# First expert of a routed layer: its first 256 rows listed after one count step instead of three

## The chip, the cores and the metric

The kernel runs on one NeuronCore of a Trainium2 chip. TensorE (PE) multiplies matrices, VectorE (DVE), ScalarE (ACT) and GpSimd (POOL) work on tiles, SyncE (SP) issues plain DMAs; GpSimd issues the indirect DMAs that gather and scatter rows. Each engine takes its own instructions in the order of the program, and semaphores tie the engines together. The metric is the device time of one execution in microseconds.

## The reference

Windowed attention (8 sequences of 576 positions, 8 heads of 64, a window of 128 with a distance bias) gives x, 4608 rows of 512. Then comes a layer of eight experts with a fixed capacity:

```python
N, D = x.shape
E = w_gate.shape[1]
cap = N // E
logits = x @ w_gate
flat = logits.flatten()
order = np.argsort(-flat)
...
for idx in order:
    tok, e = (int(idx) // E, int(idx) % E)
    if assigned[tok] >= 0 or counts[e] >= cap:
        continue
    assigned[tok] = e
    counts[e] += 1
...
for e in range(E):
    mask = assigned == e
    h = np.maximum(x[mask] @ w1[e], 0.0)
    out[mask] = h @ w2[e]
```

All 36864 pairs of a row and an expert are taken in the order of their logits; a row goes to the first expert that still has room, and each expert takes exactly 576 rows. Which expert fills first, and with which rows, is known only when all logits are.

## The kernel before, in words

**Routing** runs in eight phases (`Router.phase`). A phase finds the threshold at which the next expert fills: rows are held as 36 columns of 128, each row has its best expert (`OH`) and its logit (`b`). A count step places the logits into 64 bins (`place` writes `kq`), compares them with 64 bin numbers (`indicate` writes `ind`), and TensorE counts the members of every expert at every bin (matmuls `m<-OH,ind`). `enough` turns the counts into the step (`odd`, `junk`, `mx`, `sat` on VectorE, then a matmul `m<-sat,c_ones`), and `lo`, `w` hold the narrowed interval. Phase 0 does three such steps, of which most of the first is counted during attention (only the last ten columns are left for its end). A matmul `m<-T,c_ones` then gives the totals of the experts (`Dc`), VectorE names the expert (`ei`), and the list of its 576 rows is made: running sums (`run`, `ex`), positions by two matmuls, one-hot codes (`hif`, `hv`, `hOH`, `slo`, `mv`, `loOH`), 18 matmuls `m<-mv,loOH`, and `io`, `ia`, `idx`. The later phases count candidates in another way (`few`, matmuls `m<-OHf,ind`) and end with the same list.

**An expert.** Five gathers of 128 rows (the last of 64) fetch x by `idx` (`g`). TensorE turns each tile (four transposes into `pg` or `po`: a flip), ScalarE casts it (`xh`) and VectorE takes the remainder (`xl`). The weights come as four chunks of 512 KB a layer (`raw`, four buffers). ScalarE casts each (`hl`, 1024 columns) and VectorE takes two remainders of 512 columns (`hl`; here called splits). Layer 1 multiplies xh by both parts of the weights and xl by the high part: 192 matmuls into `ph`; ScalarE applies the ReLU (`hh`) and VectorE takes its remainder (`hlo`, and a short `hh`). For the first expert layer 1 runs over columns 0 to 255 for all eight blocks of 128 hidden units and then over columns 256 to 575; the other experts take two halves of 288 together, block by block. Layer 2 has 112 matmuls into `po`, tile by tile; ScalarE copies the result and GpSimd scatters it.

**Order.** Routing of phase 0 is written in program order on VectorE and TensorE. Elsewhere a scheduler places instructions from the order in which the code was recorded. `slot` is called at the steps of a layer's generator and hands out routing steps, loads, splits and flips by the tables `W_LOAD` and `W_SPLIT`, so the routing of the next expert but one runs beside the layers of an expert. Around the first expert the order is set by `issue_after` and by zero matmuls (`keep_warm`, 24 of them), which occupy TensorE while it has nothing else. The request of the first expert's weights (`loads`) reads `ei` into a register of SyncE; chunks 2 and 3 wait for a copy `late` behind the first flips.

## Time and profile before

| | us |
|---|---|
| median of three runs | 691.48 |
| lowest and highest run | 691.15, 692.19 |
| the profiled execution | 692.76 |
| its span | 691.0 |
| first matmul of layer 1, first expert | 231.03 |
| first matmul of layer 1, second expert | 295.08 |

A row of the chain of waits gives the start, the duration and the work in it. A row of a timeline gives the start, the time, the engine, the line, the operation, what it writes and reads, shapes and a count; in brackets stands the engine's idle time before it and what ended that. Where a helper records every operation (the line L456 or, in the changed program, L461), one looks at the names of the tiles. The numbers behind a group of names are busy times, not intervals: matmuls overlap, so their mean time is longer than the step from one to the next.

### The profile page before, as it was taken

To read this page: it belongs to the slowest core of one execution; us is meant where nothing else is said; L and a number is where in the kernel's file an instruction comes from. 1 tells how busy PE (TensorE), PEld (TensorE's weight loads), DVE (VectorE), ACT (ScalarE), POOL (GpSimd) and SP (SyncE) were. 2 spreads that over 40 slices of the span, in tenths; PEclk is the share of its full clock that TensorE was granted. 3 is DMA by queue.
4 is the path that set the end of the run, shared out by engine and by line. 5 is a ranking of instruction groups with operands and counts; after the bars stand their busy time and mean duration, and the time that the engine had idled before them with its cause. 6 is when DMAs were issued, how large, how long until landed. Compare 5 with 4: busy or idle time off the path is not lost.

```text
span 691.0 us, 18850 instructions
## 1 busy us (share of the span) xinstructions
PE 660.8 (96%) x7266; PEld 581.2 (84%) x7267; DVE 453.4 (66%) x1876; ACT 325.1 (47%) x991; POOL 152.4 (22%) x337
## 2 busy tenths in 40 slices
...
GB/s 313 139 205 206 195 227 173 219 179 223 109 90 80 228 25 251 121 131 191 74 206 102 93 132 158 45 123 183 55 114 172 104 92 152 110 30 39 1 25 49
DMA packets 35138, 92.71 MB, mean 134 GB/s; under 512 B 3808, under 2 KB 13152, under 8 KB 35040
## 3 DMA queue, kind: packets, MB, share of 16 engines
...
q8 instruction: 59, 0.97, 0.6%
q14 instruction: 39, 0.32, 0.2%
...
## 4 chain that ended last, share of the span: by engine, by line
PE 85%; DVE 7%; DMA 4%; ACT 2%; issue 1%; SPq 0%; POOL 0%; POOLq 0%; DVEq 0%
PE ph L954 26%; PE po L983 10%; PE po L984 10%; PE po L986 8%; PE s L53 7%; PE x L53 7%; PE pt L53 7%; PE pt L160 6%; PE pg L931 2%; DMA raw<-in_w_dram 2%; DVE hl L898 1%; ACT hl L896 1%; ACT u L147 1%; PE m L589 1%; DMA rel_sb<-in_rel_dram 1%
## 5 line engine op out<-in xcount | busy, mean ns | idle before, releaser
L954 PE MATMUL ph<-xh,hl 128*128 128x288 f32 (+2 forms) x1024 | 189.8, 299 | 0.0
L954 PEld LDWEIGHTS ph<-xh,hl 128*128 128x128 f32 x1024 | 154.3, 189 | 1.0
L983 PE MATMUL po<-hl,hh 128*128 128x512 f32 (+1 forms) x328 | 130.8, 399 | 0.0
L147 ACT ACTIVATE u<-u,mn 128x192 f32<-128x192 f32 (+2 forms) x288 | 124.0, 438 | 5.5 <-DVE mn L137 5.5
L984 PE MATMUL po<-hl,hh 128*128 128x512 f32 (+1 forms) x328 | 126.5, 386 | 0.0
L954 PE MATMUL ph<-xl,hl 128*128 128x288 f32 (+2 forms) x512 | 115.7, 298 | 0.0
L960 ACT ACTIVATE hh<-ph 128x288 fp32r<-128x288 f32 (+2 forms) x128 | 46.8, 408 | 144.6 <-PE ph L954 144.3
L986 PE MATMUL po<-hl,hlo 128*128 128x512 f32 (+1 forms) x264 | 102.1, 387 | 0.0
L898 DVE TENSOR_TENSOR hl<-raw,hl 128x512 fp32r<-128x512 f32 x128 | 84.9, 682 | 13.7 <-ACT hl L896 13.2
L137 DVE CUSTOM_DVE_ANT_0 u<-s,bm 128x192 f32<-128x192 f32 (+1 forms) x248 | 71.8, 346 | 32.4 <-PE s L53 31.7
L995 POOL DMA_INDIRECT out_dram<-o,idx x40 | 44.6, 1116 | 204.2 <-ACT o L990 125.0
L954 PEld LDWEIGHTS ph<-xl,hl 128*128 128x128 f32 x512 | 84.1, 189 | 0.1
L935 DVE TENSOR_TENSOR xl<-pg,xh 128x512 fp32r<-128x512 f32 (+1 forms) x37 | 23.7, 640 | 83.0 <-ACT xh L934 82.9
L965 DVE SCALAR_TENSOR_TENSOR hlo<-ph,hh 128x288 fp32r<-128x288 f32 (+2 forms) x128 | 49.8, 417 | 39.7 <-ACT hh L960 39.5
L896 ACT CAST hl<-raw 128x1024 fp32r<-128x1024 f32 x64 | 65.5, 1049 | 17.1 <-DMA raw<-in_w_dram 12.1
L983 PEld LDWEIGHTS po<-hl,hh 128*128 128x128 f32 x328 | 61.8, 188 | 11.1
L984 PEld LDWEIGHTS po<-hl,hh 128*128 128x128 f32 x328 | 61.9, 189 | 10.6
L990 ACT COPY o<-po 128x512 f32<-128x512 f32 (+1 forms) x33 | 18.9, 573 | 95.5 <-PE po L986 60.5
L907 POOL DMA_INDIRECT g<-x,idx x40 | 43.4, 1086 | 83.4 <-PE pg L931 33.8
L53 PE MATMUL s<-qk 64*64 64x192 f32 (+1 forms) x992 | 60.5, 327 | 0.6 <-DMA qk<-in_qk_dram 0.3
L986 PEld LDWEIGHTS po<-hl,hlo 128*128 128x128 f32 x264 | 49.6, 188 | 10.1
L147 ACT ACTIVATION_READ_ACCUMULATOR u<-u,mn 128x1 f32 x288 | 55.8, 194 | 0.0
...
## 6 DMA issues: line engine op xcount, KB each, us to landing
...
g<-x,idx POOLq DMA_INDIRECT x40, 3.4
out_dram<-o,idx POOLq DMA_INDIRECT x40, 2.8
```

The costliest lines, as they stand in the source:

```text
L53: put(nc.tensor.matmul(out, w, a, start=start, stop=stop, skip_group_check=True))
L137: put(nc.vector.tensor_tensor_reduce(out=weights(n, t, h), in0=x[:, c:c + 64 * m].rearrange("q (j k) -> q j k", k=64), in1=bm[n % NP][:, y ...
L147: put(nc.scalar.activation(u, u, AF.Exp, bias=st["mn"][:, i:i + 1], scale=-1.0, accum_out=st["sm"][:, i:i + 1]))
L896: self.last = nc.scalar.copy(hl[:, 0, :], raw)
L898: nc.vector.tensor_tensor(hl[:, 1, c:c + 512], raw[:, c:c + 512], hl[:, 0, c:c + 512].bitcast(F32), ALU.subtract)
L954: nc.tensor.matmul(pp[t], w[:, a, j, fo:fo + 128], x[:, j, cut[t]:cut[t + 1]], start=(j == 0 and a == 0 and x is xh), stop=(j == 3 and a = ...
L960: nc.scalar.activation(o, pp[t], AF.Relu)
L965: nc.vector.scalar_tensor_tensor(d, pp[t][:, c0:c1], 0.0, o[:, c0:c1].bitcast(F32), ALU.max, ALU.subtract)
L983: nc.tensor.matmul(out, a, wh, start=(f == 0), stop=False)
L984: nc.tensor.matmul(out, a, wl, start=False, stop=(f == 7 and t == 4))
L986: nc.tensor.matmul(out, hl[:, f, 128 * t:128 * t + 128], wh, start=False, stop=(f == 7))
L995: self.sent = nc.gpsimd.indirect_dma_start(out=self.out, out_offset=bass.IndirectOffsetOnAxis(ap=idx[:r, t:t + 1], axis=0), in_=o[:r, :], ...
```

## The change

The changed program makes two lists for the first expert. After the first of the three count steps, `first_full` takes the expert whose count stays at 576 or more up to the highest bin as the guess, and the rows of it that lie above that bin within the first 28 columns; the first 256 of these are listed (`idxa`). With the guess in a register of SyncE three chunks of weights are requested, and two gathers fetch the 256 rows. The other two count steps follow; what they select, less the rows listed already (`rest`), gives a second list of 320 rows for three more gathers. Layer 1 runs first over the 256 columns, then over the 320, and layer 2 over all five tiles. A flag is set if the second list has not exactly 320 rows or if the expert is another; then the exact path computes everything over again. VectorE, TensorE and ScalarE get their order from the program in this part (`OrderedCore` with `scalar`), in layer 2 TensorE alone (`OrderedTensor`). The routing of the second expert starts in the second half of layer 1 and runs in layer 2 by the table `ROUTE_2`, in 40 steps of layer 2; its gathers are issued at step 30 and its flips stand at steps 36, 37, 38 and 40. The routing of the third expert starts with the second expert. There are 13 zero matmuls instead of 24. The diff, cut to its core:

```diff
-EARLY = 4
-AHEAD = (18, 0, 0)
-EARLY0 = 1
-SOON, HI0 = 2, 1
+AHEAD = 18, 0, 0
+ZEROS = 1, 4, 1, 3, 4
+CHOICE_1 = {1: 1, 4: 1, 6: 1}
+LOWS_2 = {3: 2, 5: 2, 6: 2, 7: 2}
+ROUTE_2 = 11, 13, 15, 17, 19, 21, 22, 25, 29
+GATHER_2, TURN_2 = 30, (36, 37, 38, 40)
+LOAD_2 = {24: 2, 30: 1, 34: 1}
+SPLIT_2 = 33, 35, 37, 39
...
+AHEAD_COLS, AHEAD_ROWS = 28, 256
...
+    def first_full(self, cnt, more, key, am, w, low):
+        nc, rt, C = self.nc, self.p["rt"], self.C
+        n = AHEAD_COLS
+        odd, total = rt.tile([J, 8], F32, name="odd"), rt.tile([J, 8], F32, name="junk")
+        nc.vector.tensor_tensor(odd, cnt[J:2 * J, 8:16], more[J:2 * J, :], ALU.add)
+        nc.vector.tensor_tensor(total, cnt[0:J, 0:8], odd, ALU.add)
+        full = rt.tile([J, 8], BF, name="fo", bufs=1)
+        nc.vector.tensor_scalar(full, total, float(CAP), None, ALU.is_ge)
+        g = self.bank()
+        nc.tensor.matmul(g[:, 0:8], C["ones"][0:J, :], full, start=True, stop=True)
+        lo2, top, sg, mx, v = (self.small(name, k) for name, k in (("lo", 1), ("top", 1), ("sg", 8), ("kmx", 1), ("of", 1)))
+        nc.vector.tensor_reduce(top, g[:, 0:8], AX.X, ALU.max)
+        nc.vector.scalar_tensor_tensor(sg, g[:, 0:8], 8.0, C["e8"], ALU.mult, ALU.add)
+        sel = rt.tile([128, NT], BF, name="sel")
+        nc.vector.tensor_scalar(sel[:, 0:n], key[:, 0:n, 0], top[:, 0:1], None, ALU.is_ge)
+        nc.vector.tensor_reduce(mx, sg, AX.X, ALU.max)
+        nc.vector.scalar_tensor_tensor(v, top, -8.0, mx, ALU.mult, ALU.add)
+        m, ex = self.members(am, v[:, 0:1], sel, n)
+        nc.vector.tensor_scalar(self.guess, v, -1.0, 8.0, ALU.mult, ALU.add)
+        nc.vector.scalar_tensor_tensor(lo2, w, top[:, 0:1], low, ALU.mult, ALU.add)
+        return lo2, m, ex, v
+    def ahead_hits(self, m, ex):
+        nc, n = self.nc, AHEAD_COLS
+        sp = self.bank()
+        self.positions(sp, m, ex, n)
+        some = self.some = self.p["rt"].tile([128, NT], BF, name="some_m", bufs=1)
+        nc.vector.scalar_tensor_tensor(some[:, 0:n], sp[:, 0:n], float(AHEAD_ROWS), m[:, 0:n], ALU.is_lt, ALU.mult)
+        return self.hits(sp, some, n, 2, self.nc.scalar)
+    def ahead_rows(self, hits):
+        self.rows(self.bank(), hits, AHEAD_COLS, 2, self.few_rows)
+        r = self.rest[:, 0:AHEAD_COLS]
+        self.nc.vector.tensor_tensor(r, r, self.some[:, 0:AHEAD_COLS], ALU.subtract)
...
+        cnt = self.count(ind, OH, c0, NT)
+        w2, low = self.small("w"), self.small("low")
         nc.vector.tensor_tensor(low, lo, w, ALU.subtract)
         nc.vector.tensor_scalar(w2, w, 1.0 / J, None, ALU.mult)
+        self.place(cl, lo, rw, 0, c0, key)
+        rw2 = self.small("rw")
         nc.vector.tensor_scalar(rw2, rw, float(J), None, ALU.mult)
-        n = yield from n
-        lo2 = self.small("lo")
-        nc.vector.scalar_tensor_tensor(lo2, w, n[:, 0:1], low, ALU.mult, ALU.add)
-        return lo2, w2, rw2
+        lo, m, ex, v = self.first_full(cnt, self.part, key, am, w, low)
+        w, rw = w2, rw2
+        key = self.place(cl, lo, rw)
+        hits = self.ahead_hits(m, ex)
+        for s in (1, 2):
+            ind = rt.tile([128, NT, J], BF, name="ind", bufs=1)
+            for i, (a, z) in enumerate(self.halves(0, NT)):
+                if s == 1 and i == 0:
+                    self.indicate(ind, key, a, z)
+                    self.ahead_rows(hits)
+                    yield
+                else:
+                    self.indicate(ind, key, a, z)
+            low = self.small("low")
+            nc.vector.tensor_tensor(low, lo, w, ALU.subtract)
+            if s == 1:
+                w2, rw2 = self.small("w"), self.small("rw")
+                nc.vector.tensor_scalar(w2, w, 1.0 / J, None, ALU.mult)
+                nc.vector.tensor_scalar(rw2, rw, float(J), None, ALU.mult)
+            yield
+            cnt = self.count(ind, OH, 0, NT)
+            yield
+            n = self.enough(cnt, self.pen)
+            next(n)
+            yield
+            try:
+                next(n)
+            except StopIteration as e:
+                n = e.value
+            if s == 1:
+                lo2 = self.small("lo")
+                nc.vector.scalar_tensor_tensor(lo2, w, n[:, 0:1], low, ALU.mult, ALU.add)
+                lo, w, rw = lo2, w2, rw2
+                key = self.place(cl, lo, rw)
+        sel, rest = (rt.tile([128, NT], BF, name=name, bufs=1) for name in ("sel0", "rsel"))
+        nc.vector.tensor_scalar(sel, key[:, :, 0], 1.0, n[:, 0:1], ALU.add, ALU.is_ge)
+        nc.vector.tensor_tensor(rest, self.rest, sel, ALU.mult)
+        nc.vector.scalar_tensor_tensor(self.hi, w, n[:, 0:1], low, ALU.mult, ALU.add)
+        m, ex = self.members(am, v[:, 0:1], rest, NT)
...
+        idx = rs.tile([128, 5], I32, name="idx", bufs=4)
+        self.rows(self.bank(), hits, NT, 3, idx)
+        self.idx[0] = [self.few_rows[:, t:t + 1] for t in range(2)] + [idx[:, t:t + 1] for t in range(3)]
+        yield
...
+    go()
+    raw = ask(r.guess, 0, range(3))
+    rows = [r.few_rows[:, t:t + 1] for t in range(2)]
+    ga = m.gather(rows, range(2), m.x[0:128 * AHEAD_COLS, :])
+    m.idle = P["ps_h"].tile([128, 512], F32, name="ph")
+    W = [m.high(raw[c]) for c in range(2)]
+    go(2)
+    m.keep_warm(ZEROS[0])
+    m.low(W[0], raw[0], 0)
+    go()
+    m.keep_warm(ZEROS[1])
+    m.low(W[0], raw[0], 1)
+    go(2)
+    m.low(W[1], raw[1], 0)
+    a0 = m.flip(*ga[0], "o")
+    m.keep_warm(ZEROS[2])
+    go()
+    a1 = m.flip(*ga[1])
+    m.keep_warm(ZEROS[3])
+    go()
+    m.under(*a0)
+    m.under(*a1)
+    late = marked(0)
+    raw += ask(late, 0, (3,))
+    second = ask(late, 1, (0,))
+    m.keep_warm(ZEROS[4])
+    m.hidden()
+    go()
+    layer(0, 0)
+    m.low(W[1], raw[1], 1)
+    layer(1, 0)
+    W.append(m.high(raw[2]))
+    go()
+    gb = m.gather(r.idx[0], range(2, 5))
+    rest(0, 0)
+    go()
+    for half in range(2):
+        m.low(W[2], raw[2], half)
+    layer(2, 0)
+    W.append(m.high(raw[3]))
...
+    late = marked(1)
+    second += ask(late, 1, range(1, 4))
...
+    V, lows = [], []
+    for f in range(8):
+        layer(f, 1)
+        if f == 0:
+            go()
+        if f % 2 == 0:
+            V.append(m.high(second[f // 2]))
+            lows += [(V[-1], second[f // 2], half) for half in range(2)]
+        if f:
+            rest(f - 1, 1)
+        for _ in range(CHOICE_1.get(f, 0)):
+            next(route)
+        for _ in range(LOWS_2.get(f, 0)):
+            m.low(*lows.pop(0))
+    rest(7, 1)
+    return V
...
-    with tc.issue_after(r.last.ins):
-        for _ in range(EARLY0):
-            next(route)
-    W = {(0, 0): [m.split(raw[c]) for c in range(HI0)]}
-    with tc.issue_after(r.last_pe.ins):
-        m.idle = P["ps_h"].tile([128, 512], F32, name="ph")
-        m.keep_warm(WARM0)
-    tn = m.turn(g, True)
-    with tc.issue_after(m.last.ins):
-        next(tn)
-    with tc.issue_after(m.turned.ins):
-        late = P["rt"].tile([1, 1], I32, name="late")
-        last = tc.nc.vector.tensor_copy(late, r.ei[0][0:1, 0:1])
-    raw += list(m.loads(late, 0, range(SOON, 4)))
-    with tc.issue_after(m.last.ins):
-        for _ in range(TURN0 - 1):
-            next(tn)
-    W[0, 0] += [m.split(raw[c]) for c in range(HI0, 4)]
-    with tc.issue_after(last.ins):
-        for _ in range(EARLY - EARLY0):
-            next(route)
...
+        V = first_expert(tc, P, C, r, m, route)
+        r.nc = m.nc = OrderedTensor(tc)
+    i = 0
+    for _ in m.layer2(V, m.h, r.idx[0], fine=True):
+        i += 1
+        if i in ROUTE_2 and not exact:
+            next(route)
+        if i == GATHER_2:
+            gathers[0] = m.turn(m.gather(r.idx[1]))
+        for _ in range(LOAD_2.get(i, 0)):
+            load(1, 0)
+        if i in SPLIT_2:
+            part(1, 0)
+        if i in TURN_2:
+            next(gathers[0])
+    while len(W[1, 0]) < 4:```

Three places show how the order moves. On VectorE, behind the first count step, where `hl` is the split of a weight chunk of the first expert and `idxa` the early list; before:

```order
L456 TENSOR_SCALAR kq<-c_74,lo,rw 128x72
L456 TENSOR_TENSOR ind<-kq,c_i_425 128x1152 x2
L456 TENSOR_TENSOR low<-lo,w 128x1
L456 TENSOR_SCALAR w<-w 128x1
L456 TENSOR_SCALAR rw<-rw 128x1
L456 TENSOR_TENSOR odd<-m,pen 64x8
L456 ISA junk,mx<-m,odd 64x8
L456 ISA mx 64x1
L456 TENSOR_SCALAR sat<-mx 64x1
L456 SCALAR_TENSOR_TENSOR lo<-w,m,low 128x1
L456 TENSOR_SCALAR kq<-c_74,lo,rw 128x72
L456 TENSOR_TENSOR ind<-kq,c_i_425 128x1152 x2
```

and now:

```order
L461 SCALAR_TENSOR_TENSOR idxa<-ia 64x2 x2
L461 TENSOR_TENSOR rest<-rest,some_m 128x28
L461 TENSOR_TENSOR ind<-kq,c_i_429 128x1152
L461 TENSOR_TENSOR low<-lo,w 128x1
L461 TENSOR_SCALAR w<-w 128x1
L461 TENSOR_SCALAR rw<-rw 128x1
L461 TENSOR_TENSOR hl<-raw,hl 128x512
L461 TENSOR_TENSOR odd<-m,pen 64x8
L461 ISA junk,mx<-m,odd 64x8
L461 ISA mx 64x1
L461 TENSOR_SCALAR sat<-mx 64x1
L461 TENSOR_TENSOR hl<-raw,hl 128x512
```

Between the second count's indicators and its sum `odd` stands a split now, and another one between `sat` and the next `lo`.

On TensorE, at the end of the first expert's layer 2, where the flips of the second expert (`pg<-ident_sb,g`) stand; before, one flip and what follows it:

```order
L986 MATMUL po<-hl,hlo 128x512
L525 MATMUL m<-ed,craw 128x1
L931 MATMUL pg<-ident_sb,g 128x128 x4
L983 MATMUL po<-hl,hh 128x512
L984 MATMUL po<-hl,hh 128x512
L986 MATMUL po<-hl,hlo 128x512
```

and now:

```order
L461 MATMUL po<-hl,hh 128x512 x8
L461 MATMUL pg<-ident_sb,g 128x128 x4
L461 MATMUL po<-hl,hh 128x512 x2
L461 MATMUL pg<-ident_sb,g 128x128 x4
L461 MATMUL po<-hl,hh 128x512 x2
L461 MATMUL pg<-ident_sb,g 128x128 x4
L461 MATMUL po<-hl,hh 128x512 x4
L1105 MATMUL ph<-xh,hl 128x288
L461 MATMUL pg<-ident_sb,g 128x128 x4
```

The flips stood far apart, each followed by many matmuls of layer 2; now four of them stand within nine matmuls, the fourth one behind the first matmul of the second expert's layer 1.

On ScalarE, at the same place, where `hl` is the cast of a weight chunk of the second expert, four of layer 1 and then those of its layer 2, and `xh` the cast of a turned tile; before:

```order
L896 CAST hl<-raw 128x1024 x3
L990 COPY o<-po 128x512
L934 CAST xh<-pg 128x4x128
L896 CAST hl<-raw 128x1024 x2
L990 COPY o<-po 128x512
L934 CAST xh<-pg 128x4x128 x2
L990 COPY o<-po 128x512
L934 CAST xh<-pg 128x4x128
L990 COPY o<-po 128x512
L934 CAST xh<-pg 128x4x64
```

and now:

```order
L1036 CAST hl<-raw 128x1024 x3
L1154 COPY o<-po 128x512
L1036 CAST hl<-raw 128x1024
L1078 CAST xh<-pg 128x4x128
L1036 CAST hl<-raw 128x1024 x2
L1078 CAST xh<-pg 128x4x128
L1036 CAST hl<-raw 128x1024
L1078 CAST xh<-pg 128x4x128
L1036 CAST hl<-raw 128x1024
L1078 CAST xh<-pg 128x4x128
L1111 ACTIVATE hh<-ph 128x288
L1078 CAST xh<-pg 128x4x64
```

Two casts of layer-2 weights stood ahead of the second `xh`; now four stand ahead of the fourth, and the copies `o` of layer 2 are past.

421 lines of the change are left out of this document (267 added, 154 removed).

## The prediction

> **What bounds the kernel now.** I read the busy times and the chain of waits first, then the busy times by stage, and then the instructions between the last attention block and the first layer of the first expert, one engine at a time. The page's busy times (span 691.0 us) and its chain by engine:
>
> ```profile
> PE 660.8 (96%) x7266; PEld 581.2 (84%) x7267; DVE 453.4 (66%) x1876; ACT 325.1 (47%) x991; POOL 152.4 (22%) x337
> PE 85%; DVE 7%; DMA 4%; ACT 2%; issue 1%; SPq 0%; POOL 0%; POOLq 0%; DVEq 0%
> ```
>
> TensorE is the bound nearly everywhere, so only stretches in which it stands still have something to give. The windows by stage (all tiles; columns: PE, PEld, DVE, ACT and POOL busy with counts, then the granted clock, the DMA share and GB/s) show where these are:
>
> ```profile
> 207.00:208.00 1.00, 0.44 (x5) 0.29 (x5) 0.78 (x6) 0.00 (x0) 0.00 (x0) 0.62 1.01 286
> 208.00:224.00 16.00, 5.31 (x64) 3.28 (x66) 12.18 (x51) 1.58 (x2) 0.00 (x0) 0.50 0.22 74
> 224.00:225.00 1.00, 1.00 (x5) 0.43 (x4) 0.91 (x2) 0.93 (x2) 0.97 (x1) 0.84 0.02 8
> 231.00:295.00 64.00, 60.41 (x415) 51.97 (x412) 52.06 (x196) 26.36 (x42) 12.28 (x12) 1.00 0.45 154
> 295.00:354.00 59.00, 57.99 (x399) 50.14 (x397) 46.21 (x176) 18.63 (x34) 17.45 (x18) 1.00 0.38 131
> ```
>
> From 208 to 224 VectorE is busy for 12.18 of 16 us with the routing of the first expert while TensorE has 5.31. This is the hole that the change works on. Behind it the first expert takes 64 us (TensorE idle 3.59) and the second 59 (idle 1.01). These two are the cover that the change draws on: VectorE is already busy for 52.06 of the 64.
>
> The hole ends as the chain tells, where the last row is the first matmul of the second expert:
>
> ```profile
> 224.03 3.51 DMA g<-x,idx
> 227.59 0.67 PE pg L931 x4
> 295.08 2.60 PE ph L954 x19
> ```
>
> **The change part by part. (1) The early list.** Today three count steps come one after the other, and then the choice, the list, the gathers. The rows of VectorE:
>
> ```profile
> 208.38 0.15 DVE L456 TENSOR_SCALAR sat<-mx 64x1 bf16<-64x1 f32 x1
> 208.80 0.22 DVE L456 SCALAR_TENSOR_TENSOR lo<-w,m,low 128x1 f32<-128x1 f32 x1 [0.28 <-PE m L456]
> 209.06 0.32 DVE L456 TENSOR_SCALAR kq<-c,lo,rw 128x72 bf16<-128x72 f32 x1
> 209.41 1.43 DVE L456 TENSOR_TENSOR ind<-kq,c_i 128x1152 bf16<-128x1152 bf16 x2
> 217.91 0.15 DVE L456 TENSOR_SCALAR ei<-ef 128x1 int32<-128x1 f32 x1
> 219.05 0.20 DVE L456 TENSOR_SCALAR hif<-m 128x36 f32<-128x36 f32 x1 [0.34 <-PE m L456]
> 220.42 1.42 DVE L456 TENSOR_TENSOR loOH<-c_i,slo 128x1536 bf16<-128x1536 bf16 x2
> 222.73 0.33 DVE L456 SCALAR_TENSOR_TENSOR idx<-ia 64x5 int32<-64x5 f32 x2
> 226.43 0.68 DVE L898 TENSOR_TENSOR hl<-raw,hl 128x512 fp32r<-128x512 f32 x1
> 230.33 0.69 DVE L935 TENSOR_TENSOR xl<-po,xh 128x512 fp32r<-128x512 f32 x1 [0.15 <-ACT xh L934]
> ```
>
> and of SyncE (requests of weights), ScalarE, GpSimd (gathers) and TensorE:
>
> ```profile
> 219.10 12.72 SPq L889 DMA_DIRECT2D raw<-in_w_dram  x4
> 223.01 2.16 ACT L896 CAST hl<-raw 128x1024 fp32r<-128x1024 f32 x2 [2.28 <-DMA raw<-in_w_dram]
> 224.03 1.18 POOL L907 DMA_INDIRECT g<-x,idx  x1 [22.18 <-DVE L L456]
> 221.43 0.85 PE L456 MATMUL m<-mv,loOH 128*128 128x40 bf16 x18 [2.42 <-DVE loOH L456]
> 222.50 4.30 PE L915 MATMUL ph<-zero 128*128 128x512 bf16 x15 [0.22 <-issue]
> 231.03 0.72 PE L954 MATMUL ph<-xh,hl 128*128 128x256 f32 x4
> ```
>
> Up to 208.80 nothing changes in time. Then come eight short VectorE steps from `top` to `ex` (0.15 to 0.25 each with their starts about 0.2 apart, like the rows from `sat` to `kq`): 1.6 us, to 210.4. `guess` is ready at 210.55. From the end of `ei` (218.06) to the first weight cast (223.01) it is 4.95 us today, so the first cast can begin at 215.5, 7.5 us sooner. `lo` and `kq` follow to 211.05. From `hif` to the end of `loOH` it is 2.79 us today for 36 columns and five tiles. With 28 columns and two tiles the big step shrinks by 1792/2304 and the one-hot steps by two thirds: an estimate of 2.5 us with `some_m`, to 213.55. Fourteen matmuls instead of 18 are 0.66 us (0.85 x 14/18), the three steps to `idxa` 0.78 (today from 222.28, the end of the 18, to 223.06): 215.0. Today the gather starts 0.97 after `idx` ends (223.06 to 224.03), so it starts at about 216.0, and its rows can be turned at 219.5 (3.51 later) rather than 227.5.
>
> **(2) What holds the early start back.** The two other count steps now run behind this list, with weight splits between them. The second count's sum `odd` stands behind the first weight split, so it waits for a transfer, a new wait for VectorE's routing: cast 215.5 to 216.55, split 0.68, `odd` at 217.25 (its counts would be there at 216.2). `sat` 217.8, split 218.5, `lo`, `kq` and `ind` 220.45, TensorE's counts 220.9. Only behind these stand the two flips, so the gathers have 1.4 us in hand. A third split, `odd` to `sat` (221.7), six short steps to `ex` (223.2) and two xl of 0.69: 224.6. I take 225.0 for the first matmul, against 231.03: **6.0 us earlier**. Bounds: 222.6 if the casts come in time and two of the splits fall into waits, 227.6 if the weights come later by 2.6 (more than half of the 4.95).
>
> **(3) The first expert.** The matmuls of a layer, from windows of the experts six and seven taken for `ph` alone (first row) and for `po` alone (second):
>
> ```profile
> 526.00:580.00 54.00, 26.12 (x192) 1.00 0.38 120
> 526.00:580.00 54.00, 26.63 (x112) 1.00 0.38 120
> ```
>
> The halves of 256 and 320 columns are there today, so layer 1 stays at 26.1. Inside it now stand 18 matmuls of the second list, the totals and three flips: 0.65 (an estimate, under the 0.85 they take at half clock), 0.3 and 2.0 (0.67 each), in all 2.95. It ends at 254.05, routing of the second expert apart. Layer 2 finds its last two weight chunks not split yet, since VectorE has two halves left (2 x 0.68) and their casts: 1.8 us of waiting, bounds 0.5 and 3.5. The totals of the second expert's routing stand behind 66 of layer 2's 112 matmuls (15.7 us) and behind that routing's range and counts, 2.46 (a whole phase is 3.58 by the windows under (5); the totals, the positions and the list, which come later, are 0.3, 0.2 and 0.62 of it): 254.05 + 1.8 + 15.7 + 2.46 = **274.0**.
>
> **(4) From there to the second expert.** What follows the totals today, in the third expert's routing (first five rows), and the first and last of the second expert's five gathers:
>
> ```profile
> 298.75 0.30 PE L700 MATMUL m<-T,c_ones 128*128 128x288 bf16 x1
> 307.67 0.74 DVE L965 SCALAR_TENSOR_TENSOR hlo<-ph,hh 128x288 fp32r<-128x288 f32 x2
> 308.34 0.21 DVE L965 SCALAR_TENSOR_TENSOR hh<-ph,hh 128x64 fp32r<-128x64 f32 x1
> 309.78 0.33 DVE L756 SCALAR_TENSOR_TENSOR idx<-ia 64x5 int32<-64x5 f32 x2
> 310.88 1.49 POOL L907 DMA_INDIRECT g<-x,idx  x1 [8.67 <-PE ph L954]
> ...
> 267.33 1.04 POOL L907 DMA_INDIRECT g<-x,idx  x1 [7.39 <-issue]
> 273.87 0.91 POOL L907 DMA_INDIRECT g<-x,idx  x1 [0.31 <-issue]
> ```
>
> Today the second expert's gathers run from 267.33 to 273.87, and its layer 1 begins at 295.08: some 18 us in hand. In the changed program they come 12.1 us (298.75 to 310.88) after totals at 274.0, less 0.8: between the steps of the list VectorE has three splits there (3 x 0.68), where today it has three rounds of hidden-layer remainders (0.74 + 0.21 each, 2.85). First gather 285.3, last 291.8 (6.5 later), landed 295.3; flip, cast and split of the short tile take 1.2 (an estimate, from 0.67 and 0.69 of a full one): 296.5. TensorE's own work from the totals on is 10.9 (46 of 112 matmuls) + 0.8 (positions and list) + 3.0 (flips) = 14.7, so without waiting it would be through at 288.7. Twelve matmuls of the next layer 1 (1.6) can run before the last tile is there, so the second expert counts as begun at **294.9**, against 295.08. Of the 6.0 us, 5.8 are spent: the wait for weights and gathers that stood ahead of the first expert comes back ahead of the second. What is queued behind it: `xh` of tiles 1 to 4 stand on ScalarE behind casts of that expert's layer-2 weights, and so behind their transfers. I price this at nothing within those 6 us of waiting, and at 3 us (three casts of 1.05) as a bound.
>
> **(5) Routing that moves back.** The windows of the tile `m` on TensorE alone (routing matmuls):
>
> ```profile
> 231.00:295.00 64.00, 5.75 (x80) 1.00 0.45 154
> 295.00:354.00 59.00, 4.96 (x76) 1.00 0.38 131
> 354.00:412.00 58.00, 3.58 (x51) 1.00 0.41 133
> ```
>
> A whole phase costs 3.58; the first expert today holds 5.75, so 2.2 us of the third expert's routing are done there. In the changed program that phase begins with the second expert. The same 2.2 us then run after 295, and no cover exists for them, TensorE being the bound: **+2.2**. From the fifth expert on the order of TensorE is the same in both.
>
> **Sum.** -6.0 for the start; +5.8 for what is lost by the second expert's start; +2.2 for routing done later: **+2.0 us**. It is made against the profiled execution (692.76, span 691.0), 1.3 us over the median 691.48; taken over to the median, 693.5.
>
> [...] By the windows the granted clock is 0.50 from 207.24 (0.62 in its first microsecond) to 224.32 (0.84 in the last), 17.1 us, and then full. TensorE had then worked without a break since 221.43, the list and 15 of today's 24 zero matmuls. The changed program has 13, but counts, flips and list stand among them from about 216. [...]
>
> **The rivals.** *The early start is kept.* If the list of the second expert comes as soon as TensorE needs it, only the 14.7 us of work follow the totals, not 20.9 (294.9 - 274.0): 693.5 - 6.2 = 687.3 us. For it: half the gathers' path is VectorE work that could go faster than in the rows quoted, since layer 2 gives VectorE nothing else but splits, and layer 2's stall may be 0.5. Against it: gather, five issues and landing alone are 10 us (6.5 + 3.5) behind a list that needs the totals first. *The weights of the second expert decide.* Eight chunks through four buffers, each freed by its splits; the casts ahead of `xh` then add the 3 us above, and the counts in layer 2 stall as today, where TensorE waited for `ind`:
>
> ```profile
> PE m L589 <- DVE ind L565: 3.1, 2, 1.8
> ```
>
> One such wait, 1.8, comes on the path: 693.5 + 3 + 1.8 = 698.3 us. It decides as soon as a layer-2 chunk lands later than the third gather. *Half clock at the start*: today the clock was back 2.9 us after TensorE's unbroken work began (221.43 to 224.32). If that work begins only with layer 1 at 225.0, the first 2.9 us run at half and 1.4 are lost: 694.9. Against it: counts and flips stand close together before. *The guess is wrong.* Then the exact path runs the experts over again, at least another 460 us (231 to 691). With the reference's inputs the first expert to fill stays the first at the finer steps, 372 of its rows are sure in the first 28 columns, and 320 remain, so I give it 1 in 100.
>
> **How the numbers follow.** This kernel's measurements can tell about 0.2% (1.4 us) from no change. Forecast (most of the gain spent, between 690 and 696): 0.46, of which half within 0.2%. Early start kept: 0.32, all faster. Weights decide: 0.14, slower. Clock: 0.07, slower. Wrong guess: 0.01. That gives faster 0.32, within 0.2% 0.23, slower 0.45. The time is the forecast's, 693.5; its own range is 690 to 696, from the bounds of (2) and (3), which rarely fall on one side. The range with 8 in 10 goes down into the first rival, to 685.5, and up to the second, 698.
>
> **What would show it.** Right: the first 256-column matmul near 225; the second expert's totals near 274; the five gathers near 285 to 292; TensorE idle for some 6 us between 285 and 297, ended by `g`; more than 4.96 us of routing matmuls in the second expert. Step (2) is wrong if `odd` does not wait for a cast, step (4) if gathers start before 280, step (5) if the second expert takes its 59 us. The forecast falls if layer 1 of the second expert runs without a break from before 291.

## The result and the profile after

The changed kernel takes 709.32 us (median of four runs, 708.26 to 710.49) against 691.84 for the kernel before: a ratio of 1.0253, 95% interval 1.0233 to 1.0273. It is slower by 17.5 us; forecast were 2.0. The profiled execution took 710.49 with a span of 708.6, so against the 691.0 of before there are 17.6 us to explain. Its busy times and its chain by engine:

```profile
PE 667.4 (94%) x7272; PEld 584.4 (82%) x7273; DVE 460.2 (65%) x1903; ACT 326.3 (46%) x992; POOL 150.3 (21%) x337
PE 79%; DVE 9%; issue 4%; DMA 4%; ACT 3%; SPq 0%; POOL 0%; POOLq 0%; DVEq 0%; ACTq 0%
```

TensorE's share of the chain falls from 85% to 79%. The windows by stage (columns as in the prediction) show that the hole ahead of the first expert is not gone but has moved behind it:

```profile
208.00:224.00 16.00, 8.34 (x70) 4.87 (x71) 11.31 (x46) 3.66 (x5) 2.20 (x2) 0.50 0.40 133
225.00:302.00 77.00, 64.80 (x401) 53.80 (x400) 54.74 (x184) 25.51 (x41) 14.81 (x15) 0.90 0.37 127
302.00:369.00 67.00, 62.32 (x405) 53.42 (x403) 46.76 (x175) 19.95 (x35) 13.02 (x13) 0.96 0.30 99
369.00:429.00 60.00, 59.41 (x411) 51.38 (x410) 46.47 (x183) 20.44 (x36) 14.73 (x16) 1.00 0.38 128
285.00:295.00 10.00, 3.02 (x14) 2.28 (x13) 4.02 (x8) 3.53 (x4) 5.65 (x5) 0.74 0.73 253
```

The first expert now spans 77 us, in 12.2 of which TensorE is idle, and the granted clock is 0.90 where it was 1.00; the second spans 67, idle for 4.7. From 285 to 295 TensorE has 3.02 of 10 us, while the DMA engines carry 253 GB/s. The first matmuls of layer 1, expert by expert, give the account:

| expert | starts, before | starts, after | length, before | length, after |
|---|---|---|---|---|
| 1 | 231.03 | 225.80 | 63.9 | 76.65 |
| 2 | 294.92 (295.08 in the chain) | 302.45 | 59.5 | 66.60 |
| 3 | 354.42 | 369.05 | 57.2 | 59.56 |
| 4 | 411.60 | 428.61 | 57.2 | 57.77 |

-5.2 for the start, +12.7 in the first expert, +7.1 in the second, +3.0 in the next two: 17.6. What TensorE waits for is in the waits by reason, first of the kernel before, where this is the only row of flips waiting for `g`, then of after (total, times, longest):

```profile
PE pg L931 <- DMA g<-x,idx: 0.8, 1, 0.8
```

```profile
PE pg L461 <- DMA g<-x,idx: 8.0, 2, 7.0
PE pg L1077 <- DMA g<-x,idx: 3.5, 1, 3.5
PE po L461 <- DVE hl L461: 1.2, 1, 1.2
```

To part work from waiting I took, for each TensorE matmul, the step to the next one's start, and as its work the lower quartile of that step over all matmuls of its kind and shape. Over four experts work goes from 220.0 to 221.1 us, and the rest (waiting and slow clock) from 17.7 to 39.5. Of that +21.8, 15.1 stand ahead of flips (0.9 to 16.1) and 4.9 ahead of layer-2 matmuls (4.4 to 9.3). So the loss is waiting and slow clock, not work.

The timeline behind the second expert's totals, ScalarE, VectorE, GpSimd and TensorE by turns:

```profile
275.24 0.28 PE L461 MATMUL m<-T,c_ones 128*128 128x288 bf16 x1
285.33 2.16 ACT L1036 CAST hl<-raw 128x1024 fp32r<-128x1024 f32 x2 [2.15 <-DMA raw<-in_w_dram]
286.42 0.69 DVE L1042 TENSOR_TENSOR hl<-raw,hl 128x512 fp32r<-128x512 f32 x1 [1.49 <-ACT hl L1036]
287.02 0.33 DVE L754 SCALAR_TENSOR_TENSOR idx<-ia 64x5 int32<-64x5 f32 x2
288.13 1.42 POOL L1058 DMA_INDIRECT g<-x,idx  x1 [8.94 <-issue]
294.12 0.91 POOL L1058 DMA_INDIRECT g<-x,idx  x1 [0.30 <-issue]
294.36 1.11 PE L461 MATMUL pg<-ident_sb,g 128*128 128x128 f32 x4 [6.98 <-DMA g<-x,idx]
295.99 1.99 ACT L1036 CAST hl<-raw 128x1024 fp32r<-128x1024 f32 x2
297.34 1.09 PE L461 MATMUL pg<-ident_sb,g 128*128 128x128 f32 x4 [1.02 <-DMA g<-x,idx]
298.47 0.59 ACT L1078 CAST xh<-pg 128x512 fp32r<-128x512 f32 x1 [0.48 <-PE pg L461]
299.83 1.11 PE L461 MATMUL pg<-ident_sb,g 128*128 128x128 f32 x4 [0.55 <-DVE xl L1084]
300.98 0.59 ACT L1078 CAST xh<-pg 128x512 fp32r<-128x512 f32 x1 [0.98 <-PE pg L461]
302.45 0.44 PE L1105 MATMUL ph<-xh,hl 128*128 128x288 f32 x1
```

Three things are to be seen. `idx` stands on VectorE behind a split that had to wait for a cast, and so for a weight chunk. The first gather, started at 288.13, can be turned only at 294.36, 6.2 us later. And then the first three flips come 2.98 and 2.49 us apart, though a flip itself is 1.1: the second waits for its gather, the third for the remainder `xl` of the tile before, which shares its PSUM bank (the memory that TensorE writes to). The weight casts between them hold nothing up here: ahead of these two `xh` ScalarE waits for the flip (0.48 and 0.98). The DMA view has the landing times, first of the kernel before (266 to 282), where the same gathers ran, then after (284 to 300):

```profile
raw<-in_w_dram SPq DMA_DIRECT2D x4, 512.0 KB, 6.0
g<-x,idx POOLq DMA_INDIRECT x5, 7.1
```

```profile
raw<-in_w_dram SPq DMA_DIRECT2D x4, 512.0 KB, 5.5
g<-x,idx POOLq DMA_INDIRECT x5, 6.2
```

So these gathers were slow before too; slack hid it, but not the 18 us of the prediction. The five tiles landed at 270.7, 274.8, 278.6, 280.8 and 281.0 and were turned at 271.1, 275.1, 279.6, 286.1 and 290.5, so the first three had 0.3 to 1.1 us in hand. The first and the third of these flips, before:

```profile
271.14 0.66 PE L931 MATMUL pg<-ident_sb,g 128*128 128x128 f32 x4
279.62 0.60 PE L931 MATMUL pg<-ident_sb,g 128*128 128x128 f32 x4
```

Where no weights moved beside them, gathers landed sooner: the first three of the first expert before after 3.5, and the fifteen of the last three experts after the change after 2.8 to 3.6.

### The profile page after: what moved, and what is told of

It is laid out like the page before. It is cut to its first block, busy times and chain, and to the rows that moved or that the text cites. A ratio compares the mean times of both kernels' runs of the same rounds, so it can differ in the third digit from the quotient of the medians.

```text
span 708.6 us, 18904 instructions
## 1 busy us (share of the span) xinstructions
PE 667.4 (94%) x7272; PEld 584.4 (82%) x7273; DVE 460.2 (65%) x1903; ACT 326.3 (46%) x992; POOL 150.3 (21%) x337
## 4 chain that ended last, share of the span: by engine, by line
PE 79%; DVE 9%; issue 4%; DMA 4%; ACT 3%; SPq 0%; POOL 0%; POOLq 0%; DVEq 0%; ACTq 0%
PE ph L1105 22%; PE po L1147 8%; PE po L1148 8%; PE pt L53 6%; PE x L53 6%; PE po L1150 6%; PE s L53 6%; PE pt L160 6%; PE ph L461 4%; PE po L461 2%; DMA g<-x,idx 2%; ACT u L147 2%; PE pg L1077 2%; DVE hl L1042 1%; DMA raw<-in_w_dram 1%
## 5 line engine op out<-in xcount | busy, mean ns | idle before, releaser
L1105 PE MATMUL ph<-xh,hl 128*128 128x288 f32 x896 | 164.3, 298 | 0.0
L1105 PEld LDWEIGHTS ph<-xh,hl 128*128 128x128 f32 x896 | 134.0, 189 | 0.9
L1147 PE MATMUL po<-hl,hh 128*128 128x512 f32 (+1 forms) x288 | 115.2, 400 | 0.5 <-ACT hh L1111 0.5
L1148 PE MATMUL po<-hl,hh 128*128 128x512 f32 (+1 forms) x288 | 111.4, 387 | 0.0
L1111 ACT ACTIVATE hh<-ph 128x288 fp32r<-128x288 f32 x112 | 40.4, 409 | 132.3 <-PE ph L1105 132.2
L1105 PE MATMUL ph<-xl,hl 128*128 128x288 f32 x448 | 97.8, 297 | 0.0
L1150 PE MATMUL po<-hl,hlo 128*128 128x512 f32 (+1 forms) x232 | 89.3, 385 | 0.0
L1042 DVE TENSOR_TENSOR hl<-raw,hl 128x512 fp32r<-128x512 f32 x112 | 73.6, 683 | 13.5 <-ACT hl L1036 13.0
L1105 PEld LDWEIGHTS ph<-xl,hl 128*128 128x128 f32 x448 | 72.4, 189 | 0.0
L1084 DVE TENSOR_TENSOR xl<-pg,xh 128x512 fp32r<-128x512 f32 (+1 forms) x35 | 22.3, 636 | 74.3 <-ACT xh L1078 74.0
L1122 DVE SCALAR_TENSOR_TENSOR hlo<-ph,hh 128x288 fp32r<-128x288 f32 x112 | 43.1, 416 | 39.6 <-ACT hh L1111 39.2
L1036 ACT CAST hl<-raw 128x1024 fp32r<-128x1024 f32 x56 | 57.4, 1049 | 20.4 <-DMA raw<-in_w_dram 16.1
L1154 ACT COPY o<-po 128x512 f32<-128x512 f32 (+1 forms) x33 | 18.9, 574 | 103.2 <-PE po L1150 51.6
L1147 PEld LDWEIGHTS po<-hl,hh 128*128 128x128 f32 x288 | 54.5, 189 | 10.5 <-ACT hh L1111 0.7
L1148 PEld LDWEIGHTS po<-hl,hh 128*128 128x128 f32 x288 | 54.6, 189 | 9.4
L1058 POOL DMA_INDIRECT g<-x,idx x38 | 40.4, 1062 | 72.1 <-PE pg L1077 22.9
L160 PE MATMUL pt<-ident_sb,u 128*128 128x128 f32 x368 | 52.8, 279 | 0.7 <-ACT u L147 0.4
## 6 DMA issues: line engine op xcount, KB each, us to landing
raw<-in_w_dram SPq DMA_DIRECT2D x64, 512.0 KB, 4.2
x<-xb SPq DMA_DIRECT2D x14, 512.0 KB, 3.6
```

Of the source, the lines that this page charges most:

```text
L160: put(nc.tensor.transpose(ps[:, c:c + 128], u[:, o + 128 * j:o + 128 * j + 128], ident))
L1036: self.nc.scalar.copy(hl[:, 0, :], raw)
L1042: self.nc.vector.tensor_tensor(hl[:, 1, c:c + 512], raw[:, c:c + 512], hl[:, 0, c:c + 512].bitcast(F32), ALU.subtract)
L1105: self.nc.tensor.matmul(pp[t], w[:, a, j, fo:fo + 128], x[:, j, cut[t]:cut[t + 1]], start=(j == 0 and a == 0 and x is xh), stop=(j == 3 an ...
L1122: self.nc.vector.scalar_tensor_tensor(d, pp[t][:, c0:c1], 0.0, o[:, c0:c1].bitcast(F32), ALU.max, ALU.subtract)
L1147: nc.tensor.matmul(out, a, wh, start=(f == 0), stop=False)
```

## The experiments

Four kernels first, beside one another. The list's wait and the transfer beside the gathers were the two suspects. Behind each expectation stand the ratio to the kernel before with its 95% interval and, as the start, the first matmul of the second expert. The names that the expectations use for runs stand in brackets in the headings.

**The second expert's gathers freed from its list** (they read the first expert's; `e1_gather_free`):

```diff
-            gathers[0] = m.turn(m.gather(r.idx[1]))
+            gathers[0] = m.turn(m.gather(r.idx[0]))
```

> Edit: the five gathers of the second expert read the first expert's list instead of its own, at the same step of layer 2; its weights are still requested by its own choice, and its routing still runs. (The rows that the second expert works on are therefore the wrong ones; nothing else changes.) The second expert's layer 1 starts at 302.45 in the changed kernel. Theory LIST (the list comes too late, behind totals at 275.2, and that alone holds the flips): the gathers are issued near 276 to 283, land before step 36, TensorE waits at most for weights, layer 1 starts near 292 and the whole takes about 699 us. Theory WEIGHTS (the transfers of the second expert's weights and their casts and splits in the same 15 us are as bad): the start comes only to 296 to 298, the whole to about 704.

1.0129 (1.0088 to 1.0171); the second expert starts at 295.82. The last gather is now issued at 242, so no flip waits for one, and still the start is later than before the change: the flips come 2.1 to 3.1 us apart and wait for `xl`. The list and its landing are about half of the loss, not all of it. (The kernel before ran in every batch of runs, with medians of 692.76 to 694.53 us on the five chips of these experiments, so kernels of different batches are compared by their ratios to it.)

**The same, and the weights' request freed too** (`e1_list_free`):

```diff
-            loaders[e, layer] = m.loads(r.ei[e], layer)
+            loaders[e, layer] = m.loads(r.guess if e == 1 else r.ei[e], layer)
```

> Edit: as e1_gather_free, and the second expert's weights are requested by the first expert's guess, so that neither gathers nor weights wait for its routing. (It then works with the wrong rows and weights; all the work is still done.) Both theories expect the stall of about 9 us ahead of the second expert to go: layer 1 starts near 290 (totals at 275 and 14.7 us of TensorE's own work behind them). What it tells apart is the rest: if the late list of the second expert is all that went wrong there, the whole takes 697 us, and 5 us over the kernel before remain for the third expert and later; if it ends at 691 or below, the trouble of the third expert was only a consequence of the second.

1.0208 (1.0167 to 1.0248), start 299.40: worse than the half of it. With the weights there early, casts and splits stand ahead of the routing on VectorE (the totals come at 281.0, not 275.2), and layer 2 waits 3.0 for its own splits instead of 1.2. A miss for both theories: an earlier arrival can cost time by the order on VectorE and ScalarE.

**Layer-2 weights requested behind the last flip** (through a copy of the register `ei`, ordered behind `xl`; `e2_late_w2`):

```diff
+        with tc.issue_after(m.turned.ins):
+            lates[1, 1] = P["rt"].tile([1, 1], I32, name="late2", bufs=1)
+            nc.vector.tensor_copy(lates[1, 1], r.ei[1][0:1, 0:1])
-            loaders[e, layer] = m.loads(r.ei[e], layer)
+            loaders[e, layer] = m.loads(lates.get((e, layer), r.ei[e]), layer)
```

> Edit: the second expert's layer-2 weights are requested only behind the remainder of its last turned tile, by a copy of its number (as the kernel before does for two chunks of the first expert). Theory LIST: the gathers land as late as before, the start of layer 1 moves by less than 1 us, 708 to 710 us. Theory WEIGHTS: the first gather takes some 3.8 us instead of 6.2, the casts no longer stand ahead of the turned tiles, layer 1 starts near 298 instead of 302.45, and the whole takes about 705 us.

1.0168 (1.0127 to 1.021). The rows of this kernel, gather, flip and `xh` by turns:

```profile
285.37 1.00 POOL L1058 DMA_INDIRECT g<-x,idx  x1 [7.25 <-PE po L461]
288.76 0.66 PE L461 MATMUL pg<-ident_sb,g 128*128 128x128 f32 x4 [2.45 <-DMA g<-x,idx]
289.46 0.59 ACT L1078 CAST xh<-pg 128x512 fp32r<-128x512 f32 x1 [2.73 <-PE pg L461]
290.08 0.69 DVE L1084 TENSOR_TENSOR xl<-pg,xh 128x512 fp32r<-128x512 f32 x1 [2.03 <-issue]
290.82 0.66 PE L461 MATMUL pg<-ident_sb,g 128*128 128x128 f32 x4 [0.94 <-issue]
294.31 0.31 PE L1105 MATMUL ph<-xh,hl 128*128 128x288 f32 x1
```

Without weights beside it (none move from 285.3 to 289) the gather lands within 3.4 us, not 6.2: that the weights slow the gathers is shown. Flip, `xh`, `xl` and the next flip follow one another without a break, 2.06 us a round: one PSUM bank `pg` serves all flips. The second expert starts 8.1 us sooner. Not all of it is the edit's: `idx` is there at 284.26 instead of 287.02. In the profile of the changed kernel the cast of the second weight chunk starts 3.2 us after that of the first, and the list waits for it; here and in four other kernels with the same requests (the first, the next two and the one with zero matmuls) it starts 1.2 to 1.7 us after, so that wait looks like chance of one run. And only some 6 us arrive at the end: at the third expert's flips the wait grows from 3.5 to 4.7.

**The second expert's splits placed behind its list** (`e3_split_behind`):

```diff
+        hl = m.high(raw)
+        with tc.issue_after(r.last.ins):
+            for half in range(2):
+                m.low(hl, raw, half)
```

> Edit: the splits of the second expert's layer-1 weights are placed behind its list on VectorE. In the changed kernel three of them stand between the steps of the list, and the last of these waits for a cast until 286.4, so the list ends at 287.35. Without them it should end near 284.5, and all five gathers come 2.5 to 3 us sooner. Theory LIST: the whole becomes 2.5 us faster, about 707 us. Theory WEIGHTS: the gathers then run beside still more of the weights, and 1 us or less is gained.

1.0158 (1.0118 to 1.0198): `idx` at 283.77 instead of 287.02, gathers at 284.88, start at 297.10. By the ratios the order of VectorE ahead of the list is worth about as much as the landing; the intervals can't tell the two apart.

**Both together**, the two edits above (`c1_both`):

> Edit: e2_late_w2 and e3_split_behind together (second expert: layer-2 weights requested behind its last turned tile, splits of its layer-1 weights behind its list). Alone they moved the start of its layer 1 from 302.45 to 294.3 and 297.1. Theory ONE WAIT (both shorten the same wait for the gathers): together 291 to 292 and about 701 us on the scale where the changed kernel takes 709.3. Theory TWO WAITS (list and queue add up): 289, and 697.

1.0178 (1.0146 to 1.0211), start 295.36. The parts alone are worth 0.85 and 0.95%, both together 0.75%: they don't add, and the start agrees with neither theory. The flips still come 2.1 to 2.7 us apart, and the third expert's wait for its gathers is now 5.3. So there are more waits in a row behind the first one. The next four kernels build on this one.

**The third expert's routing at every step** instead of at the scheduler's pace (`c2_fast`):

```diff
-        if st["wait"] <= 0 and (k + 1 not in r.idx or k + 2 not in r.idx and i >= AHEAD[min(k, 2)]):
+        if (st["wait"] <= 0 or k == 1 and 2 not in r.idx) and (k + 1 not in r.idx or k + 2 not in r.idx and i >= AHEAD[min(k, 2)]):
```

> Edit: c1_both, and in the second expert a routing step is taken at every step of its layers until the third expert's list is there, instead of at every second or third. Its totals then stand some 18 matmuls of layer 1 and the list some 23 of layer 2 earlier. Theory BACKLOG (the second expert takes 65 to 68 us instead of 59.5 because the third expert's list is begun a whole expert later than before and its flips wait): the wait of 3 to 5 us at the third expert's first flip goes, the second expert takes 61 to 62, and the whole is 4 us faster than c1_both. Theory VECTOR (VectorE cannot do routing and splits faster there): less than 1 us.

1.0112 (1.0081 to 1.0142); that wait falls from 5.3 to 0.8. The backlog of the third list is a part of the loss, 0.66%, as the theory of the backlog had it.

**And the second expert's routing six steps earlier in layer 2**, with its loads, gathers and splits (the tables, with the flips at 33, 35, 37, 39; `c3_early`):

```diff
-ROUTE_2 = 11, 13, 15, 17, 19, 21, 22, 25, 29
-GATHER_2, TURN_2 = 30, (36, 37, 38, 40)
+ROUTE_2 = 5, 7, 9, 11, 13, 15, 16, 19, 23
+GATHER_2, TURN_2 = 24, (33, 35, 37, 39)
```

> Edit: c2_fast, and in the first expert the second expert's routing is recorded six steps of layer 2 earlier (and its three steps of layer 1 earlier too), with gathers at step 24, loads and splits six steps earlier, flips at 33, 35, 37 and 39. The totals then stand behind 48 of the 112 matmuls instead of 66. Theory BACKLOG: the totals come 3 to 4 us earlier, layer 1 of the second expert starts 3 to 4 us earlier than in c2_fast, and the whole gains as much. Theory VECTOR: VectorE still splits layer-2 weights then, TensorE waits at the counts instead, and the gain is under 1 us.

1.0069 (1.0044 to 1.0094): totals at 271.1, the first flip at 285.99 waits for no gather, start at 291.48. The first four flips stay 2.0 to 2.1 us apart. The intervals of this kernel and the one before it just overlap, but they shared a chip, and their runs do not (697.61 to 699.66, and 700.58 to 702.03).

**And three steps of the third routing in the first expert** (30, 34, 38 added to `ROUTE_2`; `c4_three`):

> Edit: c3_early, and three steps of the third expert's routing recorded in layer 2 of the first expert (at steps 30, 34 and 38), where TensorE waits anyway. The third expert's totals then stand some 74 matmuls of layer 1 earlier (about 10 us). Theory BACKLOG: the second expert's excess over 59.5 us (7.8 in c3_early) falls to 3 or 4, the whole is 3 to 4 us faster than c3_early, within 1 us of the kernel before. Theory VECTOR: the steps push the splits of the second expert's weights back, its start is 2 us later and the gain at most 2 us.

1.0068 (1.0046 to 1.0091): nothing gained. The first expert about keeps its length (64.8, from 65.6), and the second grows to 70.4 (from 67.3).

**Gathers of the second and of the third expert freed from their lists**, with both parts (they read the first expert's list; `x_free2`):

```diff
-                gathers[k], st["turn"] = m.turn(m.gather(r.idx[k + 1])), i + TURN_WAIT
+                gathers[k], st["turn"] = m.turn(m.gather(r.idx[0 if k == 1 else k + 1])), i + TURN_WAIT
```

> Edit: c1_both, and the gathers of the second and the third expert read the first expert's list, so that they wait for no routing (wrong rows, all work still done; weights by their own routing). It shows what the early start is worth when the later lists don't matter. Theory EARLY START (the 5.2 us gained at the first expert are real and only the late lists eat them): 687 to 690 us on the scale where the kernel before takes 691.8. Theory NO GAIN (the fixed order costs TensorE as much inside the first expert as the start gives): 692 to 695.

1.0106 (1.0067 to 1.0144). With no list in the way of either expert, more than 1% is still lost; neither theory had said so. Here flips wait 2.4 us for `xl`.

**Zero matmuls against the half clock** (`e4_warm`). After the change the clock is at half from 289.77 to 303.42. In this kernel 30 zero matmuls (the row shows 29) stand ahead of the second expert's first flip:

```diff
+        if i == TURN_2[0] and not exact:
+            m.idle = P["ps_h"].tile([128, 512], F32, name="ph")
+            m.keep_warm(30)
```

> Edit: the changed kernel with 30 zero matmuls (0.215 us each at full clock) ahead of the second expert's first flip, where TensorE waits 7 us. Theory CLOCK (the half clock from 289.8 to 303.4, which the wait brings on, costs by itself): the flips and matmuls from 294 to 303 run at full clock, the second expert starts 2 to 3 us sooner, 706 to 707 us where the changed kernel takes 709.3. Theory WAIT ONLY (ScalarE, VectorE and the gathers set these steps, not TensorE's pace): under 1 us.

1.0272 (1.0242 to 1.0302): no gain. Its rows:

```profile
288.03 6.42 PE L461 MATMUL ph<-zero 128*128 128x512 bf16 x29
294.29 0.60 PE L461 MATMUL pg<-ident_sb,g 128*128 128x128 f32 x4
296.63 1.04 ACT L1036 CAST hl<-raw 128x1024 fp32r<-128x1024 f32 x1 [1.04 <-DMA raw<-in_w_dram]
297.58 0.58 ACT L1078 CAST xh<-pg 128x512 fp32r<-128x512 f32 x1
299.05 0.66 PE L461 MATMUL pg<-ident_sb,g 128*128 128x128 f32 x4 [3.71 <-DVE xl L1084]
```

The first flip takes 0.60 instead of 1.11, so the clock was full (0.91 on the mean from 286 to 306: up to the second expert it was at half only for 3.41 us, from 300.65). But the `xh` behind it waits on ScalarE behind casts, these for weights, and the second flip comes 4.8 us after the first. In the changed kernel these casts stood behind the first `xh`, which began 1.15 us after its flip; and the first gather, started at 286.80, is turned only when the zeros end. So the edit moved more than the clock, and it doesn't price the half clock. The rounds of flips do, as an estimate: one that waits for the bank alone takes 2.49 us at half clock (297.34 to 299.83 in the changed kernel) and 2.06 at full, so the half clock costs some 0.4 us a flip, a small part of the loss.

**Two PSUM banks for the flips**, on top of both parts (odd tiles go to the pool of `po`; `b1_two_banks`):

```diff
-            self.under(*self.flip(h, g, r))
+            self.under(*self.flip(h, g, r, "o" if two and h % 2 else "g"))
```

> Edit: c1_both, and the second expert's tiles 1 and 3 are turned into a bank of the pool that layer 2 writes to, so that successive flips don't share one bank. Theory BANK (each flip waits for the remainder of the tile before, 2.06 us apart in c1_both): the flips come about 1.2 to 1.5 us apart, as the gathers land, the second expert's layer 1 starts 2 us sooner and the whole is 2 us faster than c1_both. Theory GATHERS (they are issued 1.3 to 1.8 us apart, and that sets the pace): under 0.7 us.

1.012 (1.0094 to 1.0145), against 1.0178 with one bank. The rows of TensorE:

```profile
286.74 0.66 PE L461 MATMUL pg<-ident_sb,g 128*128 128x128 f32 x4 [1.50 <-DMA g<-x,idx]
288.53 0.63 PE L461 MATMUL po<-ident_sb,g 128*128 128x128 f32 x4 [0.67 <-DMA g<-x,idx]
290.07 0.63 PE L461 MATMUL pg<-ident_sb,g 128*128 128x128 f32 x4 [0.44 <-DMA g<-x,idx]
291.47 0.63 PE L461 MATMUL po<-ident_sb,g 128*128 128x128 f32 x4
291.85 0.38 PE L1105 MATMUL ph<-xh,hl 128*128 128x288 f32 x1
```

The flips now come 1.8 to 1.4 us apart and wait for the gathers, which start 1.25 to 1.8 us apart, not for `xl`; the second expert starts at 291.85. The bank was a wait of its own, worth 0.58% by the ratios, whose intervals just part.

**The same on top of the earlier routing** (`c9_early_banks`):

> Edit: c3_early with the two banks of b1_two_banks. In c3_early the flips of the second expert start at 286.0 and follow each other at 2.06 to 2.7 us up to 294.8, while the gathers have landed. Theory BANK: the fifth flip comes 3 us sooner, the whole 2 to 3 us, on the level of the kernel before plus 2. Theory GATHERS: under 0.7 us.

1.0044 (1.0028 to 1.006) against 1.0069: the intervals overlap, so here the bank is probable, not shown.

**The first expert handed to the scheduler** (`c5_sched`). All the runs above keep the fixed order of the change. This one ends it behind the first two flips; layer 1 (256 columns, then 320), layer 2 and the routing of the second expert go through `slot`, as for the other experts:

```diff
+    r.nc = m.nc = nc
+    for _ in p:
+        pass
...
-    for k in range(1, E):
+        W[0, 0] = first_expert(tc, P, C, r, m, route)
+    for k in range(E):
         i = 0
-        for _ in m.layer1(W.pop((k, 0))):
+        for _ in m.layer1(W.pop((k, 0)), k == 0):
             slot(k, i)
```

> Edit: the early list and the early start of the changed kernel up to the first zero matmuls behind the first two flips; from there the order of the kernel before (the second list, layer 1, layer 2, routing, loads, splits and flips of the first expert placed by the scheduler at the kernel before's tables). The second expert's totals then stand behind 21 matmuls of layer 2 instead of 66, the third's behind 278 of layer 1 instead of 374. Theory BACKLOG (the early start is real, the fixed order behind it loses it by late routing): start near 225.5, second expert at 289 to 291, the whole 687 to 690 us where the kernel before takes 691.8. Theory LIST TWO (the second list and its gathers cost the first expert more than the early start gives): 692 to 696.

1.0116 (1.0061 to 1.017), worse than either theory. The first expert starts at 222.85, 8 us sooner than in the kernel before, and takes 74.9. Its waits for gathers:

```profile
PE pg L1078 <- DMA g<-x,idx: 7.5, 2, 4.2
```

**And a routing step at every slot** (`c6_sched_fast`):

```diff
-        if st["wait"] <= 0 and (k + 1 not in r.idx or k + 2 not in r.idx and i >= AHEAD[min(k, 2)]):
+        if (st["wait"] <= 0 or k <= 1 and k + 1 not in r.idx) and (k + 1 not in r.idx or k + 2 not in r.idx and i >= AHEAD[min(k, 2)]):
```

> Edit: c5_sched, and in the first two experts a routing step at every step of the layers until the next expert's list is there. The third expert's totals then stand where they stand in the kernel before or a little later (244 against 218 matmuls of layer 1). Theory BACKLOG: another 1 to 2 us under c5_sched. Theory VECTOR: no change, or up to 1 us slower, because routing then comes ahead of splits.

1.0113 (1.0085 to 1.0141): no gain; the first expert takes 78.4 us, 3.5 more, and the second 62.9.

**Late weights under the scheduler** (`c8_late_weights`). Layer-2 weights of the first two experts are requested behind their flips, and the second list's flips are written at step 6 of layer 1 and use two banks:

```diff
+            if k == 0 and i == 6 and not exact:
+                for _ in first:
+                    pass
+                lates[0, 1] = after_turn(r.guess, 1)
...
+            if k == 0 and not exact:
+                lates[1, 1] = after_turn(r.ei[1], 2)
```

> Edit: c5_sched, with the first expert's layer-2 weights requested only behind its last turned tile, and the second expert's too, so that no weights travel beside the gathers that TensorE waits for; the second list's three flips are recorded behind seven of the eight blocks of the first half (in c5_sched they stood behind four and TensorE waited 3.4 us), and its second tile uses another bank. Theory QUEUE: the gathers land in 3.5 to 4 us, the waits of 3.4 and 4.3 us at the flips go, the second expert starts at 289 to 291 instead of 297.7 and the whole takes 691 to 694 us on the scale where the kernel before takes 691.8. Theory LATE WEIGHTS: the splits of the late weights stop layer 2 instead, and less than 3 us are gained over c5_sched.

1.0028 (1.0005 to 1.0052), 0.9% better than without, and the best of all these. The first expert takes 66.9 us, and its waits for gathers are down from 7.5 to

```profile
PE pg L1078 <- DMA g<-x,idx: 1.4, 1, 1.4
```

The edit holds three things; which of them did how much was not taken apart.

**Its third expert's routing moved into the first expert** (`c10_ahead`, `c11_ahead2`, `c12_ahead3`). Three kernels, which change the condition that hands out routing steps: as soon as the second list is there (the first diff line), that and at every step until the third list is there (the second), and at every slot of the first expert (the third):

```diff
+        if (st["wait"] <= 0 or k == 0 and 1 in r.idx) and (k + 1 not in r.idx or k + 2 not in r.idx and i >= AHEAD[min(k, 2)]):
+        if (st["wait"] <= 0 or k == 0 and 1 in r.idx or k == 1 and 2 not in r.idx) and (k + 1 not in r.idx or k + 2 not in r.idx and i >= AHEAD[min(k, 2)]):
+        if (st["wait"] <= 0 or k == 0) and (k + 1 not in r.idx or k + 2 not in r.idx and i >= AHEAD[min(k, 2)]):
```

> Edit: c8_late_weights, and in the first expert a routing step at every step of the layers as soon as the second expert's list is there, so that the third expert's totals stand behind 2 matmuls of the second expert's layer 1 (26 in the kernel before, 97 in c8_late_weights). Theory BACKLOG: second expert 60 to 61 us, the whole 2 to 4 us faster than c8_late_weights: 689 to 692 where the kernel before takes 691.8. Theory VECTOR (VectorE is full in the first expert, routing pushes the splits and remainders back): the first expert gets as much longer, no gain.

> Edit: c10_ahead, and the same in the second expert until the third expert's list is there. Theory BACKLOG: like c10_ahead or up to 1 us faster, because the fourth expert's totals come earlier too. Theory VECTOR: slower than c10_ahead by 1 us or more.

> Edit: c10_ahead, but a routing step at every step of the first expert from its beginning, so that the second expert's list too comes 8 matmuls earlier and its flips stand 12 to 31 matmuls earlier. Theory BACKLOG: up to 1 us faster than c10_ahead. Theory GATHERS: the flips then stand ahead of the landing of the gathers again and TensorE waits there, 2 us slower.

1.0039 (1.0017 to 1.0061), 1.0039 (1.0017 to 1.0062) and 1.0044 (1.0021 to 1.0068): none better than the one they start from. First expert 69.1, 69.0 and 68.6 (66.9 there), second 62.0, 64.5 and 62.7 (63.1): what one gains the other pays.

No version beats the kernel before. For the best one the same account as above says why: its first expert starts 8.5 us sooner (222.54); over four experts it has 2.9 us more work (222.9 against 220.0) and 6.5 more of waiting (24.2 against 17.7). Together 9.4, and the fifth expert starts 0.9 us late. The rest of its span's 2.4 lies behind that, mostly in the last expert (59.0 against 57.1), and there behind TensorE's last matmul: 7.5 us against 5.7, while that matmul itself ends 0.55 later (685.87 against 685.32). In the twenty traces of this case this end takes 5.7 to 5.9 us ten times and 7.0 to 7.7 ten times, with the same copy and scatter, so it isn't the edit's; it also blurs differences of 0.2 to 0.3% between single kernels here. That the 6.5 are VectorE's load is argued from the last three runs and not shown; as a share VectorE is hardly busier (55.22 of 67 us in that first expert, 52.06 of 64 in the kernel before: 82 and 81%).

## Why the prediction was wrong

The sign was right, the size was not: +2.0 forecast, +17.6 measured by the spans, above the range's 698. The miss of 15.6 us is 0.8 at the start, 0.4 in step (3), 6.3 in step (4) and 7.9 in step (5); 0.2 come from the second expert's start before, 295.08 in the chain and 294.92 by its first matmul. The rows of after that steps (1) and (2) rest on:

```profile
213.90 2.18 ACT L461 CAST hl<-raw 128x1024 fp32r<-128x1024 f32 x2 [3.12 <-DMA raw<-in_w_dram]
214.00 1.18 POOL L1058 DMA_INDIRECT g<-x,idxa  x1 [13.51 <-DVE ind L461]
214.98 0.69 DVE L461 TENSOR_TENSOR hl<-raw,hl 128x512 fp32r<-128x512 f32 x1 [0.89 <-ACT hl L461]
215.71 0.17 DVE L461 TENSOR_TENSOR odd<-m,pen 64x8 f32<-64x8 f32 x1
223.13 0.25 DVE L461 TENSOR_SCALAR sel<-kq,m 128x36 bf16<-128x36 bf16 x1 [3.07 <-PE m L461]
225.80 0.78 PE L461 MATMUL ph<-xh,hl 128*128 128x256 f32 x1
```

**(1) The early list** comes even sooner: the gathers forecast at 216.0 start at 214.00, and the first weight cast begins at 213.90 (215.5). The landing was wrong already here: 4.9 and 4.1 us, beside three weight chunks, for 3.51. It did no harm, because the flips stand behind the counts.

**(2) The early start** is right in its number, 225.80 against 225.0, and partly by luck. `odd` does stand behind a cast and a split, but comes 1.5 us sooner than forecast (215.71 for 217.25), and 2.3 us are lost behind it: VectorE waits 3.07 us for the matmul that sums `sat` of the last count, which TensorE reaches only behind two flips and four zeros at half clock. That wait was not in the sum. The half clock, left out of the sum and kept as a rival, did come: it lasts from 204.44 to 228.33, so the first 2.5 us of layer 1 run at half speed.

**(3) The first expert up to the totals** is right: the wait of layer 2 for splits is 1.2 (1.8), the totals come at 275.24 (274.0), 49.4 us behind the first matmul for 49.0.

**(4) From there to the second expert** is the first step that failed. It gave 20.9 us from totals to the second expert; it takes 27.2. By the sum's own path, the first gather comes after 12.9 us (11.3), the last lands 11.0 later (10.0), and layer 1 begins 3.3 behind that instead of 0.4 ahead of it: 1.6 + 1.0 + 3.7. The first of these is a split before `idx` whose cast waits for its chunk; in the run with late layer-2 weights the first gather comes 11.2 after the totals, so this part looks like chance. Behind the other two stand two things. The landing: the first gather's took 6.2 instead of 3.5, a price taken from the first expert's first gathers, which run without weights beside them (3.5 each for three). The row that bears on it, the second expert's own gathers at 267 to 274, was quoted for its start times alone; their landing times, 3.3 to 8.2 us, were not read. And the flips: the sum let all but the last go while later gathers land; they begin with the first landing (294.31) and go at the pace of landings, of one bank and of the half clock, 2.5 to 3 us a round, so that from there to the second expert's first matmul are 8.1 us. The casts ahead of `xh`, set to nothing with 3 us as a bound, did cost nothing here.

With no weights under way a gather took 3.4 us (in the run with late layer-2 weights); the five beside four weight requests took 5.0 to 7.4. So the landing taken in step (4) was that of a gather alone; how the weights slow it is not shown.

**(5) Routing that moves back** named the right work and the wrong price, and is the second step that failed. Routing matmuls on TensorE, by the windows of `m` for the first three experts:

```profile
226.00:302.00 76.00, 4.46 (x70) 0.90 0.37 129
302.00:369.00 67.00, 5.24 (x71) 0.96 0.30 99
369.00:429.00 60.00, 5.48 (x82) 1.00 0.38 128
```

The first holds less than before (5.75), the second 0.3 more (4.96) and the third 1.9 more (3.58), together the 2.2 of the sum. But the price is a wait, which the sum put at nothing: the third expert's list is late, and the chain through 330 to 372 goes over its gather:

```profile
344.86 6.64 DMA g<-x,idx
351.54 1.11 PE pg L1077 x4
```

Where the list came faster this wait was gone (5.3 to 0.8) and 0.66% with it, some 4.6 us. So +2.2 became +10.1 (7.1 + 3.0); what the rest of it consists of is not shown.

**The rivals.** "The weights of the second expert decide" (698.3) named the right culprit by another mechanism: casts ahead of `xh` and one wait for `ind`. That the weights slow the gathers, and the bank, were not in it. "The early start is kept" did not happen in any version that was run. The guess of the expert held. The half clock behind the first expert, 13.65 us from 289.77, was in no rival. By the rounds of flips it costs some 0.4 us a flip; the run with zeros, which moved ScalarE's order too, can't tell what full clock alone would be worth.

The prediction's own sign was there: TensorE idle ended by `g`, forecast for some 6 us, is 7.0 in the first wait alone.

**What the 2.5% consist of**, as far as edits took it away, each on top of the one before: landing and order of splits 0.75 (2.53 to 1.78), pace of the third list 0.66 (to 1.12), second list six steps earlier 0.43 (to 0.69), second bank about 0.25 (to 0.44). Each is a difference of ratios that are known to 0.2 to 0.3 on either side. These shares go by the order of the edits: the bank taken right after the first was worth 0.58. The last 0.44 (0.28 to 0.6) stays open.
